# Spill transfers in 256 KB halves, last sums on half of the rows, fewer magnitudes on VectorE, and a new order

## The chip, the cores and the metric

One core of a Trainium2 chip runs the kernel: TensorE (PE in the profile), VectorE (DVE), ScalarE (ACT), GpSimd (POOL), and SyncE (SP), which here only issues transfers. The metric is the device time of one execution in microseconds. The time before is the median of three runs.

## What is computed

Two state-space convolutions, A and B, of one input u (2048 x 512), mixed by a gate. For each of 512 channels d, the kernel K is a sum over 128 complex states:

```python
    logdA = dt * A                     # A = A_re + 1j * A_im, dt = exp(log_dt)
    P = jnp.exp(logdA[:, :, None] * l[None, None, :])            # l = 0 .. 2047
    K = jnp.einsum("dn,dnl,dn->dl", Cc, P, dB).real
    ...
    Kf, Uf = rfft(K padded to 2L), rfft(u padded to 2L)
    y = irfft(Uf * Kf)[:L] + u * Dskip
...
x = A_u
g = sigmoid((x * gate_w).sum(-1, keepdims=True))
out = g * A_ref(x) + (1 - g) * B_ref(x)
```

(The names of the reference are kept; padding and transposes are shortened.)

## The kernel before

All of it is float32. The 512 channels are cut into 8 chunks of 64, and a chunk has 128 columns, 64 of model A and 64 of B. A column's kernel K over 2048 positions is the product of two small tables over the 128 states, 32 and 64 positions long, so that a matmul over the states makes K. The work has these stages.

- **Steps T = 0 to 63** (`tables`, lines 543 to 596), 16 columns each, 8 to a chunk. POOL makes integer angles (tile `ang`, two products) and magnitudes (tile `mr`: a large product of 64 positions from the seeds `ml`, lines 555 to 565, and a small one of 32 from `mh`, line 566). ACT takes two sines and a square of the angles into the PSUM tiles `s` and `sq`. DVE multiplies them with the magnitudes into `ei` (imaginary part) and `mr` (real part), four instructions. PE makes K from `mr` and `ei` (`kgen`, line 588, 64 matmuls as the profile counts them), ACT or DVE copies it to `kt`. The large magnitude product is on POOL, except in every third step (T % 3 == 2), where ACT copies the 8 x 16 seeds to a PSUM bank and DVE multiplies from there.
- **First stage of the transform** (`first`, line 605): after every second step, 32 matmuls of `kt` into two PSUM banks, copied into `xa` (even chunks) or `xb` (odd ones). The same is done with u itself (tile `uin`, `u_spectra`, lines 622 to 637), two chunks at a time; then the second stage of u's transform goes to tile `z` and is stored in DRAM as `us`: eight parts j a pair of chunks, one store of 512 KB for each two parts.
- **Product** (`conv`, lines 674 to 694): for each chunk and j = 0 to 7, SP loads u's spectrum (256 KB, tile `u`, three buffers; for the last chunk into `ml` and `mh`), PE makes the second stage of K's transform (line 618) and DVE multiplies both into `y` (line 690).
- **Way back** (`back`, lines 696 to 729): for each two parts, U = 0 to 3, 64 matmuls (line 710) into two banks, two copies x = 0, 1 into `z`, a store of 512 KB into the DRAM tile `zb` and a load of 512 KB from there into 32 of the 128 partitions of `f` (for the last chunk: `xa`). The way through DRAM turns positions into partitions. For U = 3 of the last chunk alone, both transfers were already cut in halves.
- **Last sums** (`fin`, lines 734 to 748): for each chunk, k = 0 to 3, 32 matmuls (line 742) of `f` with the gated matrices `gsi`; A and B are added in PSUM. A copy to `o` (two buffers) and an output transfer of 128 KB follow. Sum k reads the rows 8k to 8k + 7 of `f`.

Every operation is written with what it reads and writes (`Plan`, lines 153 to 198). The string `ORDER` (line 82) then lists all 1853 operations by number, in the order in which they are issued; a trailing `b` takes an operation's second engine (for a PSUM copy DVE instead of ACT, for the last outputs POOL's queue instead of SP's). Each engine works through its own operations in that order and waits where one isn't ready; so does SP with its transfers: one that waits holds up all behind it. A tile's buffers are taken in the order of the list, and an operation that opens a buffer waits for the last user of what was in it. There are four PSUM banks `c` for everything but the sines, and two buffers of `z` for stores.

The lines that the change touches: 555 (which steps), 631 to 637 (stores of u's spectrum), 685 (the loads' dependence), 716 to 729 (stores and loads of `zb`), 745 (what a last sum waits for), and the order.

Of the kernel before, what the change touches and what calls it, by code (L numbers as in the profile page):

```python
# [23 lines left out]
NB, NA = 64, 32  # L24
# [58 lines left out]
6 7 11 8 9 4 2 182 3 1 82 83 0 84 475 86 186 183 18 19 20 24 21 22 23 25 26 27 28 29 30 31 32 33 34 35 37 88 184b 185b 38 17  # L83
36 85 190 326 40 44 45 39 41 42 46 47 48 366 76 49 50 51 59 79 73 71 75 187 52 53 188 189 54 55 56 57 138 58 191 193b 61 62
67 63 60 68 192 64 69 91 14 351 87 13 218 194 15 16 98 65 70 92 93 101 94 95 89 96 43 72 66 353 77 354 78 90 74 100 99 195
102 357 104 103 105 219 113 197b 196b 198 200 355 356 221b 114 360 358 359 199 201 385 203 205 386 361 107 204 206 106 220
226 127 222 327 202 207 210 213 208 209 211 212 129 80 97 12 368 369 383 367 81 10 384 362 108 363 109 110 111 215 214 370
364 216 365 223 112 116 115 371 224 373 122 121 117 123 374 225 372 388 124 118 119 120 387 375 227 217 1403 230 125 126 128
131 134 376 228 389 136 133 231 352 132 137 135 130 5 1406 229 429 232 377 233b 244 390 378 245 391 392 393 249 394 251 395
430 250b 397 398 399 400 401 246 402 403 479 247 477 476 480 478 141 396b 404 405 406 142 143 239 144 252b 145 146 248 1414  # L90
253 148 149 234 150 151 152 407 254 240 431 416 414 427 415 154 139 140b 153 235b 155 236 418 408 379 419 420 409 237 483 417
421 422 428 410 445 446 447 147 448 241 242 156 157 432 380 381 423 159 424 435 158 436 411 433 434 437 413b 438 382 412 160
458 459 481 255 262 175 238 258 484 449 450 257 256 425 439 161 163 452 451 426 440 485 460 482 441 461 162 259 165 166 260
261 453 172 171 173 174 454 263 462 463 265b 167 164 455 168 169 612 611 464 264 609 613 177 266 179 243 176 328 330 331 290
329b 465 267 269b 268b 466 456 457 610 487 467 468 280 282 281b 469 283b 488 470b 294 284 486 170 180 499 501 616 489 502 490
491 492 471 500 442 493 518 519 516 517 494 472 444 443 503 504 495 496 506 332 275 505 473 474 531 333 507 508 520 521 509
276b 497 510 498b 522 511 532 523 524 529 533 530 277 285 278 287 270 272 286 534 535 288 525 526 536 547 549 550 548 512 537
538 334 335 608 279 289 527 336 551 539 540 552 271 553 560 562 561 554 555 528b 541 337 273 564 542 513 563 556 339 178 338
557 558 579 514 515 567 568 580 565 559 566 581 577 543 578 582 593 591 592 594 1407 1408 569 570 585 1404 544 586 583 546
584 545 340 587 588 1405 595 596 341 571 572b 598 342 1415 1426 614 618 615 573 619 599 1416 597 1425 617 181 1417 1409 1410  # L100
1411 274 1412 589 633 590 622 623 349 345 1427 600 1418 1419 601 574 602 575 576 624 603 620 621 649 347 343 625 634 626 1420
1429 635 631 632 651 652 604 348 650 744 1421 636 637 681 1428 1436 1450 1437 1422b 627 1430 628 1438 639 640 605 629 638 607
606 630 653 1413 1423 1424 1447 1439 1431 654 641 642 655 1432 643 656 657 658 662 663 664 665 666 644 679 680 645 659 695
667 1433 668 1448 660 1440 669 670 1449 682 1441 684 685 661 683 693 671 672 687 344 350 694 696 346 646 647b 1442 688 1443b
1444b 1434 1458 741 742 746 648 686 673 1459 745 674 743 1451 1435 1445 1461 689 690 691 1460 1452 692b 712 710 675 711 713
676 697 698 700 1453 701 699 678 677 714 1454 715 1455 1462 702 1446 703 717 704 1757 1763 705 725 1463 718 726 716 1764 1758
1483 1469 1470 719 723 727 724 747 751 749 706 753 754 748 752 728 729 1464 720 1471 1465b 750 1759 1765 1456 1480 1472 1466b
721 1760 1766 731 1761b 876 730 732 733 722 1767 1481 1473 878 755 707 1482 734 1474 735 708 783 709 756 757 736 1762 1457
1768 1475 1484 764 766 765 737 767 758 784 759 760 768 1476 769 1477 738 761 771 1485 740b 739b 772 770 773 1491 1467 1494
1468 1478 1502 762 1486 1487b 1488b 774 1495 1496 877 874 875 1492 1503 1493 775 785 781 795 814 782 796 815 786 763 787 776  # L110
# [3 lines left out]
835 836 810b 837 850 811 1776 848 851 1779b 856 857 849 838 852 879 858 839 883 859 880 853 860 885 886 861 1528 1519 882  # L114
1501 854 1529 862 1520 855b 863 864 1521 1010 840 884 887 897 899 900 898 1780 1777 1522 842 841b 865 1530 866 1531b 1532b
888 889 291 292 890 867 868 293 891 892 901 295 893 894 297b 296 902 869 914 916 915 904 917 870 905 903 871 872 1538 1523
298 299 918 302 1533 1534 1512 906 895 301b 907 303 921 922 305b 908 927 928 919 300 920 896b 304b 929 932 933 909 316 306
308 923 924 930 307b 309b 931 945 946 947 910 318 1784 925 935 317b 1785b 936 926b 1781 1007 934 1008 319 1009 1011 1782 977
310 937 938 978 323 321 322b 939 1786 320 1783 324b 325 1535 1006 1546 948 949 952 940b 958 959 960 961 1014 941 979 950 313
311 1790 1787 951 953 312 314 1791 962 954 975 976 911 955 965 1788 963 966 913 964 912 1539 1536 956 1540 967 989 968 942  # L120
957 980 943 981 982 1537 944b 983 991 990 1547 1548 984 1550 1541 985 1542b 986 1543b 315 1015 1549 1571 1557 1789 969 1551
1558 987 1144 1143 970b 993 1016 1012 1013 992 971 994 1559 988 995 996 997 998 972 974 973 1552 1031 1017 1020 1553 999 1032
1018 1554 1544 1560 1582 1033 1019 1029 1000 1021 1001 1561 1023 1024 1562 1572 1002 1030 1003 1022 1034 1025 1026 1573 1037
1035 1036 1005 1004 1027 1569 1047 1049 1048 1050 1060 1038 1545 1555 1579 1568 1792 1139 1556 1028 1051 1052 1563 1564 1565
1039 1040 1054 1583 1041 1053 1042 1062 1061 1043 1063 1093 1077 1094 1055 1570 1574 1580 1064 1065 1056 1067 1057 1575b
1576b 1044 1068 1584 1581 1046b 1566 1590 1140 1141 1066 1069 1142 1045 1058 1591 1059 1079 1070 1080 1592 1091 1078 1081
# [3 lines left out]
1103 1128 1275 1182 1129 1606 1130 1131 1132 1802 1613 1602 1120 1803 1133 1603 1614 1134b 1150 1104 1151 1162 1163 1152 1135  # L130
1164 1165 1153 1156 1154 1105 1801 1615 1589 1155 1107 1106 1157 1183 1179 1180 1158 1136 1607 1166 1137 1167 1138b 1169 1159
1170 1225 1608 1609 1168 1600 1623 1637 1610 1271 1616 1160 1624 1617 1184 1226 1625 1171 1618 1185 1273 1172 1619b 1620 1635
1173 1187 1634 1804 1188 1161b 1186 1272 1174b 1636 1276 1274 1626 1621 1611 1193 1227 1194 1195 1175 1196 1210 1211 1627
1176 1189 1190 1628 1191 1197 1178b 1200 1198 1177 1199 1629 1192b 1630 1631 1638 1201 1622 1648 1645 1202 1639 1203 1646
1811 1212 1213 1214 1215 1216 1812 1640 1641 1632 1670 1647 1217 1218 1219 1204 1649 1642 1220 1650 1223 1279 1224 1241 1242
1228 1231 1232 1229 1230 1814 1805 1808 1205 1809 1233 1243 1244 1254 1255 1656 1643 1813 1221 1245 1222 1246 1815 1206 1256
# [65 lines left out]
def ssm_mix(ctx: ExitStack, tc: tile.TileContext, a, out, dry=False):  # L202
# [419 lines left out]
    def u_spectra(b):  # L622
# [6 lines left out]
        for j in range(NJ):  # L629
# [205 lines left out]
```

## Time and profile before

| | us |
|---|---|
| three timed runs | 475.12, 477.8, 482.99 |
| their median | 477.8 |
| the profiled execution | 472.5 |
| its span, in which the trace's times lie | 470.7 |
| around the span | 1.8 |

The granted TensorE clock over the span is 0.971. PE is TensorE's matmuls, PEld its weight loads, SPq SyncE's queue. Transfers moved 84.5 MB, at 180 GB/s in the mean. Times of the trace count from the span's start.

### The profile page before, as it was taken

The numbers are of one execution on the slowest core, as the hardware profiler recorded it, in microseconds if no ns is written. First come the engines' busy times: TensorE is split into PE (matmuls) and PEld (weight loads), VectorE is DVE, ScalarE is ACT, GpSimd is POOL, SyncE is SP. The second block draws the span as 40 slices with busy tenths as digits, with TensorE's granted clock in tenths as the row PEclk, the third lists the DMA queues.
The fourth block names the chain that finished last, engine by engine and source line by source line (L and its number), as shares of the span: only waits on it lengthen the run. The fifth ranks groups of instructions, "written<-read, shape, count | busy, mean of one in ns | idle before, by whom it ended". The sixth has DMA issues, their size and how long they took to land.

```text
span 470.7 us, 21838 instructions
## 1 busy us (share of the span) xinstructions
PE 394.9 (84%) x9616; PEld 356.4 (76%) x9616; DVE 416.0 (88%) x518; ACT 386.2 (82%) x676; POOL 338.8 (72%) x317
## 2 busy tenths in 40 slices
PE   4797786799968879998898988879598888999935
PEld 3786685689857768787798977778587877898934
DVE  6999889999999999999899999998789999996610
ACT  3889979999988999998899999998789898791110
POOL 2593859599977989796999689878929899650010
PEclk9899899999998999999999999999999999999987
DMA  7866852836555565876465646764838667567793
GB/s 220 276 198 205 246 161 78 249 120 224 183 157 157 133 160 180 212 206 178 132 180 153 206 132 190 193 182 117 195 105 218 167 192 213 152 184 187 212 244 89
DMA packets 74542, 84.53 MB, mean 180 GB/s; under 512 B 5456, under 2 KB 60112, under 8 KB 73392
## 3 DMA queue, kind: packets, MB, share of 16 engines
q1 hardware_dynamic: 74304, 82.75, 62.0%
q8 instruction: 75, 1.23, 1.1%
q0 software_dynamic: 144, 0.39, 0.3%
q14 instruction: 19, 0.16, 0.1%
HBM read 51.48 MB, written 31.65 MB: 177 GB/s over the span
## 4 chain that ended last, share of the span: by engine, by line
PE 35%; DVE 25%; ACT 21%; issue 11%; DMA 4%; SPq 3%; DVEq 0%; POOL 0%; ACTq 0%
PE c L618 8%; PE c L605 8%; DVE mr L281 6%; PE c L588 6%; PE c L742 5%; PE c L710 4%; DVE y L690 4%; ACT s L284 4%; DVE ei L271 4%; ACT ang L284 3%; ACT sq L284 3%; SPq L289 3%; ACT ml L523 2%; DVE ei L281 2%; PE c L439 2%
## 5 line engine op out<-in xcount | busy, mean ns | idle before, releaser
L281 DVE SCALAR_TENSOR_TENSOR mr<-sq,mr 128x1024 f32<-128x1024 f32 (+1 forms) x128 | 117.4, 947 | 1.9 <-ACT sq L284 1.5
L271 POOL TENSOR_TENSOR mr<-ml 128x1024 f32<-128x1024 f32 x43 | 84.3, 1960 | 12.3 <-PE c L588 7.7
L271 POOL TENSOR_TENSOR ang<-par,cint 128x512 int32<-128x512 int32 x64 | 67.5, 1055 | 31.0 <-ACT sq L284 15.9
L271 DVE TENSOR_TENSOR ei<-s,mr 128x1024 f32<-128x1024 f32 x64 | 77.7, 1214 | 4.1 <-ACT s L284 2.8
L588 PE MATMUL c<-mr 128*32 128x64 f32 x2048 | 64.7, 223 | 14.8 <-DVE mr L281 7.3
L605 PE MATMUL c<-small,kt 128*64 128x128 f32 x1024 | 66.3, 283 | 10.9 <-issue 5.0
L690 DVE TENSOR_TENSOR y<-c,u 128x1024 f32<-128x1024 f32 x57 | 68.7, 1214 | 4.3 <-PE c L618 1.7
L284 ACT ACTIVATE s<-ang 128x1024 f32<-128x1024 int32 x64 | 65.9, 1029 | 6.5 <-POOL ang L271 4.5
L605 PEld LDWEIGHTS c<-small,kt 128*64 128x64 f32 x1024 | 58.2, 141 | 15.4 <-issue 6.3
L271 POOL TENSOR_TENSOR mr<-mh 128x512 f32<-128x512 f32 x63 | 67.7, 1080 | 2.4 <-PE c L588 2.4
L271 POOL TENSOR_TENSOR ang<-sa 128x512 int32<-128x512 int32 x64 | 68.6, 1073 | 0.2
L284 ACT ACTIVATE ang<-ang 128x1024 f32<-128x1024 int32 x64 | 67.7, 1058 | 1.2
L284 ACT ACTIVATE sq<-ang 128x1024 f32<-128x1024 f32 x64 | 66.0, 1032 | 3.2 <-DVE mr L281 2.3
L588 PEld LDWEIGHTS c<-mr 128*32 128x32 f32 x2048 | 48.6, 110 | 25.5 <-issue 9.9
L588 PE MATMUL c<-ei 128*32 128x64 f32 x2048 | 64.1, 221 | 3.2 <-issue 3.2
L710 PE MATMUL c<-y,vv 64*64 64x128 f32 x1792 | 59.9, 274 | 4.6 <-issue 2.7
L710 PEld LDWEIGHTS c<-y,vv 64*64 64x64 f32 x1792 | 50.9, 134 | 10.6 <-issue 5.2
L618 PE MATMUL c<-xa,w 128*128 128x128 f32 x384 | 52.8, 287 | 3.5 <-DVE vv L414 1.3
L618 PE MATMUL c<-xb,w 128*128 128x128 f32 x384 | 50.0, 282 | 4.7 <-DVE xb L296 1.3
L588 PEld LDWEIGHTS c<-ei 128*32 128x32 f32 x2048 | 50.6, 111 | 3.6 <-issue 3.6
L618 PEld LDWEIGHTS c<-xa,w 128*128 128x128 f32 x384 | 46.4, 194 | 7.7 <-issue 3.6
L618 PEld LDWEIGHTS c<-xb,w 128*128 128x128 f32 x384 | 45.1, 191 | 8.5 <-issue 3.1
(109 smaller groups left out, 661.9 us busy)
## 6 DMA issues: line engine op xcount, KB each, us to landing
zb<-z SPq DMA_DIRECT2D x31, 512.0 KB, 3.9
u<-us SPq DMA_DIRECT2D x57, 256.0 KB, 4.4
f<-zb SPq DMA_DIRECT2D x28, 512.0 KB, 5.2
us<-z SPq DMA_DIRECT2D x16, 512.0 KB, 3.7
uin<-in_uk_dram SPq DMA_DIRECT2D x16, 256.0 KB, 3.9
f<-in_ut_dram SPq DMA_DIRECT2D x8, 512.0 KB, 5.3
out_dram<-o SPq DMA_DIRECT2D x29, 128.0 KB, 3.2
par<-prd SPq DMA_DIRECT2D x7, 320.0 KB, 3.9
```

Of the source, the lines that this page charges most:

```text
L271: lambda e: (dve if e == "dve" else pool).tensor_tensor(out=out(), in0=in0(), in1=in1(), op=o),
L281: lambda _: dve.scalar_tensor_tensor(out=out(), in0=in0(), scalar=s, in1=in1(), op0=o0, op1=o1), reads, writes, port=port)
L284: op("act", "act", n, lambda _: act.activation(out=out(), in_=in_(), func=func, **{k: v() if callable(v) else v for k, v in kw.items()}), ...
L289: lambda e: (sp if e == "sp" else pool).dma_start(out=out(), in_=in_()), reads, writes, touch=touch)
L439: pe.matmul(t(*ps)[:, CH * i:CH * i + CH], V(x)()[:, CH * i:CH * i + CH], dgv()[:, k, i], start=True, stop=True)
L523: act.activation(out=t(*tile)[:, ks, j], in_=t("par", c)[:, 0, ks].bitcast(F32), func=AF.Exp, scale=float(l))
L588: pe.matmul(ps[32 * j:32 * j + 32, o], x[:, 4 * o + j, 64:96], x[:, 4 * o + j, 0:64], start=part == 0, stop=part == 1, tile_position=(0, 3 ...
L605: pe.matmul(t(*ps[g // 4])[64 * r:64 * r + 64, 128 * (g % 4):128 * (g % 4) + 128], t(*x)[:, g], t("small")[:, 128 * r:128 * r + 128], star ...
L618: pe.matmul(view()[:, :, k], t("w2", j // 2)[:, 4 * (j % 2) + k], t(*x1)[:, 4 * j + k], start=True, stop=True)
L690: op("dve", "tt1", 1024, lambda _: dve.tensor_tensor(out=t(*y).rearrange("p h s f d -> p h s (f d)"), in0=fv().rearrange("p s f d -> p s ( ...
L710: pe.matmul(bank_of(x)[64 * e:64 * e + 64, CH * q:CH * q + CH], v[:, 0:64] if h else v[:, 32:96], t(*ys[f // 4])[64 * x:64 * x + 64, h, :, ...
L742: pe.matmul(t(*ps)[64 * r:64 * r + 64, DC * i:DC * i + DC], t("gsi")[:, 4 * k + i, s, 64 * r:64 * r + 64], t(*f)[:, 8 * k + 2 * i + r, DC ...
```

## The change

Four things are changed.

1. Each store of u's spectrum, each store of `z` to `zb` and each load of `f` from `zb` becomes two transfers of 256 KB. A store's half leaves after its own copy x (or its own part j); a load of u's spectrum waits for its own part only; each half of a load of `f`, cut by rows (0 to 15, 16 to 31), waits for both halves of its store.
2. A last sum waits for those halves of the four loads that hold its rows: k = 0, 1 for the first ones, k = 2, 3 for the second.
3. The large magnitude product is on DVE in every fifth step (T % 5 == 4).
4. The order of all operations, now 1922, is a new one.

```diff
-        if T % 3 == 2:
+        if T % 5 == 4:
             sd = ("c", "seeds", T)
...
-            copy(512, zv, lambda ps=ps: t(*ps), [ps], [z])
-            if j % 2:
-                dma(512, lambda j=j: t("uspec", b, j // 2).rearrange("h p x -> p h x"),
-                    lambda z=z: t(*z).rearrange("p j f c -> p (j f c)").rearrange("p (h x) -> p h x", h=4), [z],
-                    [("uspec", b, j // 2)])
+            copy(512, zv, lambda ps=ps: t(*ps), [ps], [z] * (1 - j % 2) + [("uz", b, j)], touch=[z] * (j % 2))
+            dma(256, lambda j=j: t("uspec", b, j // 2)[2 * (j % 2):2 * (j % 2) + 2].rearrange("h p x -> p h x"),
+                lambda z=z, j=j: t(*z)[:, j % 2].rearrange("p f c -> p (f c)").rearrange("p (h x) -> p h x", h=2), [("uz", b, j)],
+                [("uspec", b, j)], touch=[z])
...
-        us = ("uspec", c // 2, j // 2)
+        us, stored = ("uspec", c // 2, j // 2), ("uspec", c // 2, j)
...
-        for xs in ((0,), (1,)) if end else ((0, 1),):
-            g, n = 8 * U + 4 * xs[0], 4 * len(xs)
-            dma(128 * n // 2, lambda g=g, n=n: t(*zb)[g:g + n].rearrange("g p k -> p g k"),
-                lambda xs=xs: t(*z)[:, xs[0]:xs[-1] + 1].rearrange("p x q k -> p (x q) k"),
-                [("zx", c, U, x) for x in xs], [zb] * (U == 0) + [("zu", c, U)], touch=[z] + [zb] * (U > 0))
-        for h in range(1 + end):
-            m = NA // (1 + end)
-            dma(16 * m, lambda h=h, m=m: t(*f)[32 * U:32 * U + 32, m * h:m * h + m],
-                lambda h=h, m=m: t(*zb)[8 * U:8 * U + 8].rearrange("g (m a) k -> (g m) a k", m=4)[:, m * h:m * h + m],
-                [("zu", c, U)], [f] * (U == 0) + [("fu", c, U, h)], touch=[zb] + [f] * (U > 0))
+        new = U == 0
+        for x in range(2):
+            g = 8 * U + 4 * x
+            dma(256, lambda g=g: t(*zb)[g:g + 4].rearrange("g p k -> p g k"), lambda x=x: t(*z)[:, x],
+                [("zx", c, U, x)], [zb] * (new and x == 0) + [("zu", c, U, x)], touch=[z] + [zb] * (not (new and x == 0)))
+        for h in range(2):
+            dma(256, lambda h=h: t(*f)[32 * U:32 * U + 32, 16 * h:16 * h + 16],
+                lambda h=h: t(*zb)[8 * U:8 * U + 8].rearrange("g (m a) k -> (g m) a k", m=4)[:, 16 * h:16 * h + 16],
+                [("zu", c, U, 0), ("zu", c, U, 1)], [f] * (new and h == 0) + [("fu", c, U, h)],
+                touch=[zb] + [f] * (not (new and h == 0)))
...
-        op("pe", "fin", 64, mm, [("gsi", k)] + [("fu", c, U, 0) for U in range(4)] + [("fu", c, 3, 1)] * (c == NCH - 1 and k > 1),
-           [ps], table="fin", touch=[f])
+        op("pe", "fin", 64, mm, [("gsi", k)] + [("fu", c, U, k // 2) for U in range(4)], [ps], table="fin", touch=[f])
```

What the two lists give each engine, counted from the numbers:

| | before | after |
|---|---|---|
| large magnitude products on POOL / on DVE | 43 / 21 | 52 / 12 |
| copies of seeds on ACT | 21 | 12 |
| transfers on SP / on POOL | 250 / 3 | 329 / 2 |
| copies to `o` on ACT / on DVE | 26 / 6 | 23 / 9 |
| copies to `z` on ACT / on DVE | 68 / 28 | 70 / 26 |
| copies to `xb` on ACT / on DVE | 33 / 15 | 32 / 16 |
| changes of ACT between exponential and sine | 30 | 28 |

The end of the two lists, SP's transfers of the last chunk with x or h in brackets (outputs left out before the last store). Before: store U=2, store U=3 (0), load U=1, store U=3 (1), then load U=2, load U=3 (0), load U=3 (1), and outputs. After: load U=0 (0), load U=0 (1), load U=1 (0), stores U=2 (0), (1), stores U=3 (0), (1), load U=2 (0), load U=1 (1), load U=3 (0), an output, load U=2 (1), an output, load U=3 (1), and outputs. The last two copies into `z` are both DVE's before, and ACT's and DVE's after. The last matmuls keep their sequence: products and ways back of the last chunk, with sums of the chunk before it among them, and four sums of its own at the end.

More of the change, by code (lines that the diff above doesn't have):

```diff
@@ new lines @@
+378 379 109 110 208 125 16 15 129 226 200 203 230 209 206 210 211 213 214 402 97 386 380 381 387 216 219 217 220 111 112 115
+116 389 390 113 114 121 117 122 227 123 124 118 80 399 400 119 388 228b 403 229 404 391 392 231 233 232b 215 127 212 343 221
+234 126 235 237 393 405 394 431 236b 250 251 120 412 414 415 413 135 218 128 131 132 368 406 407 408 253 256 254b 409 432
+257b 259 410 416 411b 419 420 417 130 252 133 134 136 255 495 260 418 491 238 239 492 494 141 493 148 144 421 142 422 143 423
@@ new lines @@
+149 1410 137 151 145 146 266 261 262 258 1423 240 424 150 152 139 153 140b 154 429 433 443 430 434 437 155 247 244 241 462
+395 444 445 425 446 147 164 438 435 245 436 248 242 447 396 397 156 157 448 439 440 449 163 450 451 158 460 498 461 426 428b
+427 398 464 452 453 263 160 159 161 473 463 474 496 175 270 499 264 265 441 454 465 442 455 466 162 267 165 166 268 269 467
+468 171 172 173 174 469 456 497 500 475 476 502 477 274 243 249 246 177 176 271 275 470 273b 272b 276b 471 480 167 481 472b
@@ new lines @@
+1033 984 1035 1598 985 1599 1044 1013 1057 1059 1060 1058 1036 1037 1606 1607 1047 1014 1016b 1048 1045 1600 1046 1038 1015
+1089 1039 1061 1062 1049 1050 1611 1063 1612 1051 1622 1072 1070 1071 1052 1621 1577 1017 1618 1601 1064 1065 1066 1090 1074
+1075 1613 1631 1591 1590 1858 1632 1619 1623 1067 1620 1633 1053 1073 1091 1054 1068 1614 1602 1647 1615 1634 1644 1616 1603
+1149 1151 1056 1076 1150 1069 1624 1635 1087 1088 1103 1077 1078 1079 1080 1055b 1625b 1636 1092 1081 1648 1093 1082 1095
@@ new lines @@
+1626 1865 1096 1649 1094 1097 1101 1102 1104 1156 1105 1866 1120 1083 1121 1118 1119 1637 1084 1098 1106 1638 1108 1109 1099
+1107 1110 1100b 1111 1639 1086 1122 1173 1085 1123 1578 1657 1604 1617 1871 1862 1660 1627 1867 1628 1640 1645 1125 1863b
+1126 1131 1132 1133 1154 1112 1646 1124 1872 1135 1113 1136 1157 1864 1868 1127 1128 1174 1284 1114 1115 1116 1137 1134 1138
+1139 1869b 1117b 1129 1658 1140 1158 1155 1159 1162 1130 1141 1659 1650 1142 1661 1160 1161 1163 1164 1165 1166 1143 1651
+1171 1172 1144 1175 1191 1189 1652 1176 1177 1145 1167 1662 1168 1179 1180 1641 1629 1642 1643 1873 1670 1654 1673 1280 1653
@@ L150 @@
+1405b 1379b 1762 1733 1746 1888 1761 1777 1891 1747 1758 1757 1763 1406 1407 1767 1408 1409b 1775 1768b 1776 1778 1779 1769
+1791 1788 1780 1781 1759 1771 1770 1734 1772 1773 1782 1783 1784 1760 1792 1789 1801 1804 1793 1817 1814 1805 1802 1806 1818
+1815 1794 1795 1796 1901 1807b 1902b 1808b 1797 1785 1786 1798 1809 1810 1903b 1819 1820 1907 1904 1898 1821b 1905b 1899 1822
+1823 1811 1799 1824 1906 1812 1900 1908b 1825 1909 1910 1913 1911 1914 1912b 1915 1916 1919 1917 1920 1918 1921
 """
@@ L685, in conv @@
         dma(256, lambda: uv().rearrange("p h f d -> p (h f d)"),
-            lambda: t(*us)[2 * (j % 2) + c % 2].rearrange("(q h) x -> q (h x)", h=2).unsqueeze(1).to_broadcast([64, 2, 512]), [us], uk + over)
+            lambda: t(*us)[2 * (j % 2) + c % 2].rearrange("(q h) x -> q (h x)", h=2).unsqueeze(1).to_broadcast([64, 2, 512]), [stored], uk + over)
         fv = lambda: t(*fw).rearrange("p (s f d) -> p s f d", s=2, f=4)
@@ L715, in back @@
         z, zb, f = ("z", c, U), ("zb", c), home(c)
-        end = last and U == 3
         for x in range(2):
```

85 lines of the change are left out of this document (29 added, 56 removed), and 30 rows, old and new, of the table ORDER.

## The prediction

> **What bounds the kernel now.** I read the page's busy line first, then busy time by stretch, the waits, the groups of instructions, the issues of transfers, and last the chain that ended last.
>
> ```profile
> span 470.7 us, 21838 instructions
> PE 394.9 (84%) x9616; PEld 356.4 (76%) x9616; DVE 416.0 (88%) x518; ACT 386.2 (82%) x676; POOL 338.8 (72%) x317
> ```
>
> DVE is the fullest engine, but 88% is a mean over stages that differ. Busy time in the two stretches that matter, the steady part from the ninth step's tables to the last one's, and the end (length, then busy time of PE, PEld, DVE, ACT, POOL with counts, granted clock, DMA share, GB/s):
>
> ```profile
> 102.00:425.00 323.00, 285.69 (x7596) 256.43 (x7594) 307.76 (x354) 294.96 (x491) 271.50 (x244) 0.98 0.62 172
> 425.00:471.00 46.00, 31.91 (x752) 29.82 (x752) 16.77 (x19) 6.65 (x14) 2.00 (x4) 0.89 0.70 184
> ```
>
> In the first DVE is busy 307.8 of 323 us and idles 15.2 us; ACT is at 91%, PE at 88%, POOL at 84%. So for 323 us DVE sets the pace with three engines close behind it. In the second DVE and POOL have nearly nothing left: after the last step's tables, 46 us remain that are a chain of matmuls and transfers. DVE's few idle times come from these waits:
>
> ```profile
> DVE xb L296 <- PE c L605: 5.1, 1, 5.1
> DVE ei L271 <- ACT s L284: 2.8, 4, 1.8
> DVE y L690 <- DMA u<-us: 0.6, 2, 0.4
> ```
>
> The third is the one that the transfers touch: with 64 products that each need a u load, DVE lost 0.6 us to loads that came late. The first is one single stall, looked at under the rivals.
>
> **The change part by part.**
>
> *Magnitudes.* A step's product mr<-ml runs on DVE in every third step (21 of 64) and on POOL in the others (43). With every fifth it is 12 and 52. Each product on DVE also needs a small ACT copy of the seeds into a PSUM bank. The groups (busy us, mean ns, idle before):
>
> ```profile
> L271 POOL TENSOR_TENSOR mr<-ml 128x1024 f32<-128x1024 f32 x43 | 84.3, 1960 | 12.3 <-PE c L588 7.7 <-ACT ml L523 1.7 <-issue 1.1
> L271 DVE TENSOR_TENSOR mr<-c,ml 128x1024 f32<-128x1024 f32 x21 | 25.5, 1214 | 1.5 <-ACT c L284 1.5
> L284 ACT ACTIVATE c<-ml 128x128 f32<-128x128 f32 x21 | 5.9, 281 | 0.1
> ...
> L296 DVE COPY o<-c 128x256 f32<-128x256 f32 x6 | 2.5, 417 | 17.2 <-DMA out_dram<-o 9.8 <-PE c L742 7.5
> L296 DVE COPY xb<-c 128x512 f32<-128x512 f32 x15 | 10.0, 680 | 5.2 <-PE c L605 5.1
> ```
>
> DVE loses nine products. One is 1.214 us by the group, but back to back a DVE product of that size takes less, as the chain shows:
>
> ```profile
> 125.09 1.13 DVE ei L271
> ```
>
> So 9 x 1.13 = 10.2 to 9 x 1.214 = 10.9 us come off DVE. The new order also deals the PSUM copies anew between ACT and DVE: three more o and one more xb on DVE, two spill copies fewer (the size of xb): 3 x 0.417 + 0.680 - 2 x 0.680 = +0.6 us. DVE's net is -9.6 to -10.3 us; I take -9.6, since the steady stretch runs back to back. POOL gets 9 x 1.96 = +17.6 us, ACT loses 9 x 0.281 = 2.5 us.
>
> *The order, ACT's tables.* Going down the two lists, ACT changes between its exponential and its sine tables 30 times before and 28 times after. Two loads less:
>
> ```profile
> L284 ACT ACT_TABLE_LOAD x18 | 23.1, 1283 | 1.0 <-PEq L824 0.7
> ```
>
> 2 x 1.283 = 2.6 us off ACT. By itself neither this nor the seeds' copies move the end: ACT is not the last to be waited for. It is cover for the next point.
>
> *The balance that is left.* Put on the steady stretch: DVE 307.8 - 9.6 = 298.2, POOL 271.5 + 17.6 = 289.1, ACT 295.0 - 2.5 - 2.6 = 289.9, PE 285.7 us as before. DVE still has the most, but POOL has come from 36 us below it to 9 us below. If DVE's idle time stayed at 15.2 us the stretch would lose the whole 9.6. If POOL set the pace with the same idle time, 289.1 + 15.2 = 304, it would still be shorter than 313, so POOL does not become the bound by its sum; it can only be late for single steps. When POOL is late ACT's sine waits first, and DVE behind ACT:
>
> ```profile
> ACT s L284 <- POOL ang L271: 4.5, 6, 1.8
> ```
>
> The bounds for what the tighter balance costs are 0 (all as now) and 9.6 us (everything given back). Nearest is DVE's wait on ACT's sine above, 2.8 us in 4 times with POOL at 84%; with POOL at 289.1/313 = 92% I let it double and charge +2.8 us. Steady stretch: -9.6 + 2.8 = -6.8 us.
>
> *Transfers of the spills in halves.* The 16 stores us<-z become 32; of 32 stores zb<-z and 32 loads f<-zb all but the last chunk's last pair, which is halved already, become two: 62 more. With one output moved from POOL to SP, SP issues 79 more. Issue times in ns with the landings of this tile's transfers, and the page's list of issues (count, size, median us to landing):
>
> ```profile
> L289 SPq DMA_DIRECT2D zb<-z x33: 359/376/1365, 134.7 to 451.2; - x33
> L289 SPq DMA_DIRECT2D f<-zb x28: 312/356/1414, 141.9 to 436.6; - x28
> ...
> DMA to landing us min/median/max: 3.2/4.9/7.5
> ```
>
> ```profile
> zb<-z SPq DMA_DIRECT2D x31, 512.0 KB, 3.9
> u<-us SPq DMA_DIRECT2D x57, 256.0 KB, 4.4
> f<-zb SPq DMA_DIRECT2D x28, 512.0 KB, 5.2
> ...
> zb<-z SPq DMA_DIRECT2D x2, 256.0 KB, 4.5
> xa<-zb SPq DMA_DIRECT2D x2, 256.0 KB, 5.2
> ```
>
> A half issues in the same time (33 stores, both sizes, 0.36 to 0.38 us from fastest to median) and lands no sooner (4.5 against 3.9, 5.2 against 5.2). So 79 x 0.38 = 30 us more of SP, which computes nothing, and no round trip gets shorter by size. What is won is the start: the first half of a spill leaves one copy earlier (0.68 us for one of xb's size on DVE, above). What is risked: SP issues strictly in order, and each half of an f load waits for both halves of its store; behind it stand u loads for DVE and outputs that free the o buffers. I cost all this at nothing, covered by the slack that DVE's 0.6 us wait for u shows. If that cover goes, it is the third rival.
>
> *First last-sums from the first half of the rows.* Sums k = 0, 1 of a chunk wait only for the first halves of f. For the seven chunks ahead of the last, these sums are PE filler with no one close behind: zero. For the last chunk this was already so for its last spill, which is the last to come: zero, too.
>
> *The tail.* The end of the chain (start, us, what):
>
> ```profile
> 448.69 1.30 DVE z L296 x2
> 449.99 0.51 SPq L289
> ...
> 451.16 5.34 DMA zb<-z
> ...
> 456.89 4.33 DMA xa<-zb
> 461.21 5.94 PE c L742 x128
> ```
>
> The two last copies run one after the other on DVE, 1.30 us; in the new order one is ACT's and one DVE's: 0.68, so -0.6. From the copies' end to the last store's start SP needs 451.16 - 449.99 = 1.17 us, as an earlier f load stands between the two stores; in the new order they follow one another: -0.5. Ahead of them stands f(U=1), which waits for its store to land; that store leaves four matmul groups earlier, so this is covered unless it lands late. The second half of the last f load stands three issues behind the first, 4 x 0.38 = 1.5 us, while the sums of the first half take 5.94/2 = 3.0: hidden. Two transfers in series and the 5.94 us of matmuls stay. The tail gives -1.1 us. Its other bound is +2.6: the store in front lands in this tile's maximum, 7.5, instead of its median, 4.9.
>
> *The head.* Loads come in another order, PE's and DVE's work listed ahead of the first step's tables, summed with the rows' means, is about 2 us less than before, and the loads arrive no earlier, so 0, with bounds of -2 and +2.
>
> **Sum.** -6.8 - 1.1 + 0 = -7.9 us. The profiled execution took 472.5 us (470.7 of span, 1.8 around it); it would take 464.6. The three timed runs lie at 475.1 to 483.0, median 477.8, 5.3 above the profiled one; I set the sum on the median: 477.8 - 7.9 = 469.9, about 470 us.
>
> **The rivals.**
>
> *A. All of it, and the stall too.* In the midst of 64 matmuls of the first stage PE stood 4 us with no wait:
>
> ```profile
> 333.58 2.19 PE c L605 x36
> 335.77 4.02 issue
> ```
>
> ```profile
> q8 instruction: 75, 1.23, 1.1%
> ```
>
> DVE's 5.1 us above is this stall's shadow. The instruction queue moved 75 packets, 1.23 MB; what such a packet meets among the data transfers depends on the order, so another order may not have it. With 10.3 of DVE, 5.1 and 1.1 that is 16.5 us: 461.3. For it: it happened once. Against it: more, smaller transfers are in flight in the same stretch (DMA share 0.62). The Trainium skill, page "Runtime: NRT & Kernel Launch", section "Instruction fetch mechanics", says that an engine refills its instructions in 16 KiB blocks and that the crossing is mostly hidden. 1.23 MB over 75 is 16.4 KB and agrees with the block; the 4.02 us do not agree with hidden, and by the page's rule alone this rival would be the forecast.
>
> *B. POOL takes back what DVE gives.* POOL works in order, and its four products of a step stand against the pace of the steps:
>
> ```profile
> L271 POOL TENSOR_TENSOR ang<-sa 128x512 int32<-128x512 int32 x64 | 68.6, 1073 | 0.2
> L271 POOL TENSOR_TENSOR mr<-mh 128x512 f32<-128x512 f32 x63 | 67.7, 1080 | 2.4 <-PE c L588 2.4
> L271 POOL TENSOR_TENSOR ang<-par,cint 128x512 int32<-128x512 int32 x64 | 67.5, 1055 | 31.0 <-ACT sq L284 15.9 <-DMA uin<-in_uk_dram 8.6 <-PE c L588 5.8
> ```
>
> ```profile
> L271 DVE TENSOR_TENSOR ei<-s,mr x64: 1209/1212/1226, 28.8 to 421.3; 128x1024 f32<-128x1024 f32 x64
> ```
>
> That is 1.07 + 1.08 + 1.06 + 1.96 = 5.2 us against (421.3 - 28.8)/63 = 6.2 a step. If each of the nine moved products makes its step's sine late by one POOL product of 1.07 us, and DVE with it, 9 x 1.07 = 9.6 us come back and the steady part gains nothing: with the tail 476.7. For it: 92%. Against it: POOL waits 15.9 us for ACT to free an angle buffer (the releaser in the third row), so it mostly runs ahead and has room.
>
> *C. Slower: SP's queue makes u late.* One mechanism: a u load stands behind one more issue or a half that waits, DVE's product waits, and DVE sets the pace. At 0.38 us for each of 64 products it costs 24.3 us: 477.8 - 7.9 + 24.3 = 494.2. At 0.12 us each the gain is gone, at 0.27 (17.5 us) the kernel is 2% slower. Against it: 0.6 us now, and in the new list DVE's work between a u load and its product, summed with the rows' means, has a median of 7.0 us, against 5.7 before. The Trainium skill, "DMA: Bandwidth & Descriptors", section "Anatomy of one DMA — SWDGE (gpsimd) path", gives about 2.0 us fixed for a transfer plus its bytes over 436 GB/s: an estimate of 3.2 us for 512 KB and 5.2 for two halves in series, so 78 halved transfers would carry 156 us more latency. The rows have no such gap, since the halves overlap.
>
> **How the numbers follow.** The forecast (466 to 474, middle 470) gets 0.46; A (459 to 466) 0.24; B (474 to 482) 0.19; C (over 482) 0.11. About 2%, 9.6 us, is what a measurement of this kernel can tell from no change: under 468.2 or over 487.4. Faster: A and a third of the forecast, 0.24 + 0.16 = 0.40. Slower: most of C, 0.08. Within: 0.52. The range 461 to 482 leaves out a quarter of A and C, 0.06 + 0.11; the forecast's own is 466 to 474.
>
> **What would show it.** In the steady part: DVE's mr<-c,ml x12 and POOL's mr<-ml x52 at the same means; DVE busy near 406, its idle time there near 18 us. If DVE's waits on ACT's sine or on POOL stay at 3 us, my charge was too high; near 12 us, B is right. DVE's wait for u<-us above 8 us means C. No issue stall of 4 us means half of A. In the tail: two z copies side by side, the last store's start within 1 us of the last inverse group's copies. The forecast is wrong if DVE's busy time falls by ten and the last step's tables do not end earlier.

## The result, and the profile after

The changed kernel takes 460.8 us (median; 456.7 to 462.8) where the kernel before takes 476.5 (470.5 to 483.0) in the same comparison: a ratio of 0.971 [0.966, 0.976]. Every ratio in this text (with its 95% interval) leaves out the runs over 1.5% above the fastest of their kernel, and as the runs of the kernel before spread widely, most ratios are a little above those of the medians (0.967 here). The kernel is faster, by twice what was forecast, and 0.2 us outside the range. The profiled execution took 461.8 us, 460.0 of it span; against the profiled one of before the span lost 10.7 us. That execution of before (472.5) lay near the fast end of its runs.

From the page of the changed kernel: span, busy time, the instruction queue, and the issues of transfers.

```profile
span 460.0 us, 21963 instructions
...
PE 394.3 (86%) x9616; PEld 356.7 (78%) x9616; DVE 408.9 (89%) x511; ACT 379.3 (82%) x663; POOL 355.7 (77%) x325
...
q8 instruction: 75, 1.23, 1.2%
...
zb<-z SPq DMA_DIRECT2D x64, 256.0 KB, 3.6
u<-us SPq DMA_DIRECT2D x57, 256.0 KB, 3.9
f<-zb SPq DMA_DIRECT2D x56, 256.0 KB, 4.7
us<-z SPq DMA_DIRECT2D x32, 256.0 KB, 3.4
```

DVE has 7.1 us less, POOL 16.9 more, ACT 6.9 less, where the forecast had 9.6 less, 17.6 more and 5.1 less. In the median each kind of spill transfer lands sooner than the 512 KB before (3.6 for 3.9, 4.7 for 5.2, 3.4 for 3.7 us), and so do the u loads between them, whose size did not change (3.9 for 4.4).

Busy time in the same two stretches as before, from the ninth step's tables to the last one's, and the end:

```profile
102.40:417.70 315.30, 283.00 (x7589) 254.10 (x7587) 299.48 (x342) 289.80 (x483) 285.44 (x251) 0.98 0.64 180
417.70:460.00 42.30, 31.58 (x744) 29.69 (x744) 16.33 (x20) 6.66 (x14) 1.46 (x3) 0.90 0.69 196
```

The steady stretch is 7.7 us shorter (323.0 before), the end 3.4 (45.7 from 425.0 to the span's 470.7), the head the same (102.4 for 102.0). The forecast had 6.8, 1.1 and 0. The steady part seems to come out nearly as forecast; the experiments show that this is chance, as it comes from another place.

That place shows best in the 4.02 us in which PE stood amid 64 matmuls at 335.77 us before. At this point of the program the changed kernel has (PE's instructions in order: start, us, what)

```profile
332.75 1.97 PE L607 MATMUL c<-small,kt 128*64 128x128 f32 x32
334.65 1.98 PE L711 MATMUL c<-y,vv 64*64 64x128 f32 x64
```

with no gap. The page tells what it was. PE has 9616 matmuls and 9616 weight loads, 19232 instructions; over the 75 packets of the instruction queue that is 256 each, and 1.23 MB over 75 is 16.4 KB. In the traces PE's gaps without a wait lie at every 256th of its instructions. So PE gets its instructions by DMA in blocks of 256 and stands where a block is late. The trace's records of single packets show it: ahead of each of the ten gaps of over 0.8 us before, a packet of 16,384 bytes of the instruction queue ends 1.3 to 1.5 us before PE goes on. I measure this as PE's *fetch loss*: at each 256th instruction that lies within one operation, the time from the start of the instruction ahead of it to its own, less the usual 0.03 us, summed up over the gaps that are longer than that. Before it is 19.6 us, in sixteen gaps of over 0.3 us and many small ones; after it is 8.5. The 4.02 us of the forecast's rival A were only the largest of them.

At that largest gap the packets also show what the DMA engines did meanwhile. Two loads f<-zb had been issued one behind the other, and from 332.5 to 336.5 us their packets of 16 KB hold 15 to 16 of the 16 engines. The instruction packet starts at 337.08 us, as they end, takes 1.35 us (the median of all is 1.09), and PE goes on 1.37 us later. So the packet was not slow, it started late. One thing stays open: PE had entered its last block at 329.0 us, and around 331.2 us only some 3 engines were busy; why the next block was not fetched then the trace does not show.

All kernels that ran, with the loads f<-zb as they are requested for one spill, their median landing, the fetch loss and its largest gap, the profiled span, the median, and the ratio to the kernel before in the same comparison:

```
kernel                        f requests     landing  loss  max  span   median  ratio
before                        512 KB           5.2    19.6  4.3  470.7  476.5
the change                    2 x 256          4.7     8.5  2.7  460.0  460.8   0.971 [0.966, 0.976]
after_again                   2 x 256          4.7     9.2  2.1  458.6  459.9   0.978 [0.974, 0.983]
after_third                   2 x 256          4.5     8.6  1.8  457.6  461.1   0.981 [0.974, 0.989]
old order, old magnitudes
 halves_old_order             2 x 256          4.3    10.9  1.7  460.4  467.3   0.990 [0.983, 0.996]
 f_halves_old_order           2 x 256          4.3    15.2  1.8  465.0  471.3   0.992 [0.986, 0.997]
 stores_halved_old_order      512              5.3    20.2  5.0  474.0  474.3   1.000 [0.994, 1.006]
 f_packets_old_order          512, 8 KB        5.5    24.2  3.1  475.1  478.2   1.007 [0.999, 1.015]
 f_by_partition_old_order     2 x 256          6.2    31.1  7.9  497.8  502.7   1.060 [1.049, 1.071]
 f_quarters_old_order         4 x 128          3.2     9.2  1.5  463.1  464.7   0.979 [0.975, 0.982]
 f_cut_old_order              32               2.5     6.5  1.6  461.5  463.2   0.977 [0.973, 0.981]
 quarters_halves_old_order    4 x 128          3.5     7.7  2.2  460.6  464.0   0.989 [0.985, 0.994]
old order, new magnitudes
 mags_old_order               512              5.3    18.8  2.4  476.5  479.6   1.020 [1.016, 1.025]
 mags_and_halves_old_order    2 x 256          4.3    10.4  1.7  469.8  472.8   0.999 [0.995, 1.003]
new order, new magnitudes
 whole_new_order              512              6.1    12.6  3.3  478.4  482.7   1.026 [1.021, 1.032]
 f_halves_new_order           2 x 256          4.6     9.9  2.4  463.2  464.9   0.982 [0.977, 0.988]
 f_quarters_new_order         4 x 128          3.5     4.7  1.5  459.7  459.9   0.970 [0.959, 0.980]
 quarters_new_again           4 x 128          3.7     6.9  2.0  457.9  460.2   0.980 [0.972, 0.987]
 outs_free_new_order          2 x 256          4.9     7.1  2.3  460.2  460.7   0.973 [0.967, 0.979]
```

The kernel before, in the five further comparisons, has medians of 476.7, 476.8, 474.3, 475.1 and 474.3 us, and its runs spread over 7 to 15 us. Differences under some 3 us between kernels of different comparisons decide nothing.

### The profile page after: what moved, and what is told of

Read it like the earlier page. It is cut to its first block, busy times and chain, and to the rows that moved or that the text cites. A ratio compares the mean times of both kernels' runs of the same rounds, so it can differ in the third digit from the quotient of the medians.

```text
span 460.0 us, 21963 instructions
## 1 busy us (share of the span) xinstructions
PE 394.3 (86%) x9616; PEld 356.7 (78%) x9616; DVE 408.9 (89%) x511; ACT 379.3 (82%) x663; POOL 355.7 (77%) x325
## 3 DMA queue, kind: packets, MB, share of 16 engines
q8 instruction: 75, 1.23, 1.2%
## 4 chain that ended last, share of the span: by engine, by line
DVE 26%; PE 23%; ACT 16%; issue 11%; DMA 11%; POOL 9%; SPq 3%; DVEq 0%; ACTq 0%; POOLq 0%
PE c L620 7%; PE c L607 6%; DVE mr L283 6%; DVE ei L273 5%; POOL mr L273 4%; PE c L590 4%; ACT s L286 3%; DVE y L691 3%; POOL ang L273 3%; DMA out_dram<-o 3%; PE c L711 3%; SPq L291 3%; ACT sq L286 2%; ACT ang L286 2%; DMA u<-us 2%
## 5 line engine op out<-in xcount | busy, mean ns | idle before, releaser
L273 POOL TENSOR_TENSOR mr<-ml 128x1024 f32<-128x1024 f32 x52 | 101.8, 1958 | 4.7 <-PE c L590 2.9
L711 PE MATMUL c<-y,vv 64*64 64x128 f32 x1792 | 58.1, 273 | 4.1 <-DVE y L691 1.4
L620 PE MATMUL c<-xa,w 128*128 128x128 f32 x384 | 51.3, 283 | 2.5 <-ACT z L296 1.1
L620 PEld LDWEIGHTS c<-xa,w 128*128 128x128 f32 x384 | 45.4, 191 | 6.6 <-issue 1.5
```

The source lines that it names most:

```text
L273: lambda e: (dve if e == "dve" else pool).tensor_tensor(out=out(), in0=in0(), in1=in1(), op=o),
L620: pe.matmul(view()[:, :, k], t("w2", j // 2)[:, 4 * (j % 2) + k], t(*x1)[:, 4 * j + k], start=True, stop=True)
L711: pe.matmul(bank_of(x)[64 * e:64 * e + 64, CH * q:CH * q + CH], v[:, 0:64] if h else v[:, 32:96], t(*ys[f // 4])[64 * x:64 * x + 64, h, :, ...
```

## The experiments

### One part at a time

First the change again, unaltered.

> The changed kernel once more, unaltered, for the spread of a profile. In the changed kernel's trace PE loses 8.5 us at its instruction refills (gaps at every 256th instruction, beyond the usual spacing), in the kernel before 19.6 us, and the spans differ by 10.7 us. Theory H (halved transfers shorten the refills' waits) and theory O (the new order happens to have fewer of them) both expect 461 us +- 3 and 6 to 12 us of such gaps. If the gaps are chance from one execution to the next, this run shows 15 us or more.

459.9 us: it holds. Then the change taken apart. The halves alone, in the old order and at the old places:

```diff
-            dma(16 * m, lambda h=h, m=m: t(*f)[32 * U:32 * U + 32, m * h:m * h + m],
+            dmas(16 * m, [(lambda k=k: t(*f)[32 * U:32 * U + 32, 16 * k:16 * k + 16],
...
+                           for k in ((0, 1) if not end else (h,))],
```

and the same for the stores us<-z and zb<-z: one operation of the list issues both halves, one behind the other.

> The kernel before in its own order, with each 512 KB store us<-z and zb<-z and each 512 KB load f<-zb issued as two of 256 KB at the same place. Theory H: PE's gaps at the refills fall from 20 us to about 9, and the time from 476.5 to about 466. Theory O: gaps stay near 20 us, time 476 +- 3. If more issues on SP cost anything: above 480.

467.3 us, 9.4 below before (476.7 in this comparison), where the change is 16.8 below. What the forecast costed at nothing is more than half of the gain. Busy time in the steady stretch, in the columns of above:

```profile
102.40:416.80 314.40, 282.66 (x7599) 253.36 (x7599) 307.41 (x354) 294.42 (x491) 271.52 (x244) 0.99 0.63 177
```

DVE has all of its work of before (307.4 us, 307.8 before) and idles 7.0 us in place of 15.2; its wait of 5.1 us for PE's stall is gone. Then the reverse, the new order with whole transfers; a store goes out at the place of its later half, a load at that of its earlier one:

```diff
-            dma(256, lambda h=h: t(*f)[32 * U:32 * U + 32, 16 * h:16 * h + 16],
+            once(("f", c, U), 0, 256, lambda: t(*f)[32 * U:32 * U + 32],
```

> The changed kernel in its new order, with the halves of a spill joined again into one transfer of 512 KB (a store at the place of its later half, a load at that of its earlier one). Theory H: gaps at the refills rise from 9 us to about 20, time about 471. Theory O: gaps near 9 us, time 461 +- 3, or up to 2 us more for the later stores.

482.7 us, slower than before, and outside what either theory had. Its fetch loss is only 4 us above the change's, so the larger part of these 22 us is something else: the order was made for halves, f's loads land after 6.1 us, and SP's queue stands longer behind DVE's products. Its largest wait (us in total, times, longest), first with whole transfers, then in the change:

```profile
SPq L291 <- DVE y L705: 86.4, 28, 11.8
```

```profile
SPq L291 <- DVE y L691: 55.6, 25, 8.7
```

These waits may be a cause or a mark of the lateness; that was not parted here.

Last, the magnitudes alone in the old order: nine of the 21 products go to POOL in their places.

```diff
-        if T % 3 == 2:
+        if T in (5, 11, 17, 26, 32, 38, 47, 53, 59):
+            tt("any", G * 64, lambda: t(*M)[:, :, 0:64].rearrange("p c (h l) -> p c h l", l=8),
...
+        elif T % 3 == 2:
```

> The kernel before in its own order, with 9 of the 21 large magnitude products moved from DVE to POOL at the same place and their copies of the seeds left out; transfers whole. Theory M (fewer products on DVE shorten the steady part, as the prediction had it): DVE's busy time 406, time 476.5 - 7 = 469 or less. Theories H and O: the steady part has enough other waits that less than 3 us comes of it, 474 to 478.

479.6 us, slower by 2% and above what every theory had: DVE has 8.2 us less to do, and the kernel takes longer. Where each of these gains or loses is seen in the times at which DVE ends the tables of step T (from the traces, us):

```
T     before  halves_old  f_cut_old  mags_old  mags_and_halves  the change
8     102.0   102.4       102.9      101.1     102.8            102.4
12    119.1   119.5       120.0      120.9     122.6            119.5
32    244.5   242.9       243.6      245.9     246.3            244.0
44    315.1   314.2       314.2      317.5     318.2            314.8
48    345.4   338.1       337.8      347.2     344.6            335.2
63    424.9   416.8       416.3      430.4     424.8            417.7
```

At T = 44 before, the halves and the change stand within a us of each other, whatever DVE has had to do. Between T = 44 and 48, where PE's largest fetch gap of before lies, the halves gain 6.4 us, and they hold them to the end of the tables. The kernel with the magnitudes alone is 1.8 us behind before at T = 12 and 5.5 at T = 63. In this execution the change has gained nothing over the halves alone at T = 63 (in its two other profiled ones 2.7 and 1.4 us).

### Which transfers, and which property

The loads alone in halves, and the stores alone:

> The kernel before in its own order; only the 512 KB loads f<-zb are halved, by rows of f, so that a packet has 8 KB instead of 16 KB. Theory P (a refill of PE's instructions waits behind the 16 KB packets of these loads, 1.12 us each on a DMA engine): as good as all transfers halved, about 467 us, at most 2 refills that start more than 4 us late, against 5 before. Theory S (it is the stores, or the smaller transfers as a whole): half of the gain or less, 472 to 477.

> The kernel before in its own order; only the stores us<-z and zb<-z are halved, their packets keep 512 bytes and 1 KB. Theory P: no gain, 476 us +- 3, 4 to 6 refills more than 4 us late. Theory S: 467 to 472.

471.3 and 474.3 us, where before has 476.8: the loads carry the larger part, with a ratio clear of 1, the stores' ratio is 1.000. The loads' 471.3 us lies between the two theories. Now a load in halves of 16 partitions instead of 16 rows, so that its packets stay at 16 KB:

```diff
-            dma(16 * m, lambda h=h, m=m: t(*f)[32 * U:32 * U + 32, m * h:m * h + m],
+            dmas(16 * m, [(lambda k=k: t(*f)[32 * U + 16 * k:32 * U + 16 * k + 16],
```

> The kernel before in its own order; the loads f<-zb are halved by partitions, 16 and 16, so that there are as many transfers of 256 KB as with rows halved, but each packet keeps 16 KB. Theory P: no gain, 476 us +- 3, 4 to 6 late refills. Theory T (the size of a transfer is what matters, not of its packets): about 467.

502.7 us, 26 us slower than before. I had not expected that. The chain of work through its largest fetch gap (start, us, what):

```profile
344.12 1.10 PE c L595 x64
345.23 2.19 PE c L612 x34
347.41 7.59 issue
355.01 2.18 PE c L612 x17
```

It is the matmul group of before's stall (x36, then 4.02 us), and the same place with 7.6 us. In the halves by rows PE goes through that group without a stop:

```profile
330.68 3.79 PE L612 MATMUL c<-small,kt 128*64 128x128 f32 x64
```

In the kernel by partitions, too, the 16 KB packets of these loads hold the DMA engines at that place, 15 to 16 of them from 345.2 to 351.2 us, and the instruction packet starts at 351.59. The packets' own times show why such loads block for longer (median us of one packet on a DMA engine, loads f<-zb and xa<-zb):

```
before           16 KB   1.12      f_halves    8 KB  0.59
f_by_partition   16 KB   1.79      f_packets   8 KB  0.61
whole_new_order  16 KB   1.19      the change  8 KB  0.48
```

So far a packet's length and a request's size could both be it. To tell them apart, a load of 512 KB as one request, with packets of 8 KB: the halves of a row of `f` lie apart in the tile, so that they cannot merge.

```diff
-    ring("f", 1, [128, NA, CH])
+    ring("f", 1, [128, NA * CH + 8])
...
+                lambda: t(*f)[32 * U:32 * U + 32].rearrange("p (h x) -> p h x", h=2)[:, :, 0:16 * CH],
```

> The kernel before with one thing changed: the two halves of a row of f lie 32 bytes apart in SBUF, so that a load f<-zb is still one transfer of 512 KB in its old place, but of 64 packets of 8 KB in place of 32 of 16 KB (the loads of the last chunk go to xa and stay as they were). Theory P (what costs is how long one packet holds a DMA engine, and PE's instruction fetch behind it): the gain of the halved loads, 476.7 to 471, comes without any halving: 470 to 473 us, at most two refills that start over 4 us late, PE loses 16 us or less at them. Rival R (the gain came from two transfers that are requested and land on their own): as before, 475 to 479 us, five or six late refills, some 19 us lost.

(The halves lie 16 bytes apart, 32 for the whole tile, not 32 apart as the expectation says.) 478.2 us, ratio 1.007: nothing gained, 24.2 us lost at the fetches. My theory of the packet's length fell. For loads into 32 partitions it is the request that counts: the same bytes in packets of the same length, asked for twice, gain 5 us. The page's issues of this kernel, and those of the halved loads:

```profile
f<-zb SPq DMA_DIRECT2D x28, 512.0 KB, 5.5
```

```profile
u<-us SPq DMA_DIRECT2D x57, 256.0 KB, 4.1
f<-zb SPq DMA_DIRECT2D x56, 256.0 KB, 4.3
```

The Trainium skill, page "DMA: Bandwidth & Descriptors", section "Queues, rings and completion order", says that each DMA engine takes turns between its queues by whole packets, a packet there being a run of descriptors from one ring (the profile calls each descriptor a packet). That agrees with the pair above: an instruction block waits for an engine's whole share of a request, four 8 KB pieces of 0.61 us in one request or twice two of 0.59. The traces don't say on which engine a packet ran, so this stays an agreement and is not shown, and at the largest gap of before it does not suffice, as the instruction block came behind two whole requests. The load by partitions does not follow from it alone: its share of an engine is one packet of 1.79 us, less than the whole load's two of 1.12, and its loss is the largest.

If so, still smaller requests lose still less, and a load without its bytes loses nearly nothing. Both in the old order:

> The kernel before with each load f<-zb requested as four of 128 KB, one behind the other at the old place (packets of 4 KB; those of the last chunk to xa too). Theory Q (the size of a request is what counts, down to this size): PE loses 13 us or less, 466 to 470 us, less than the halves' 471. Rival H (the gain is had with two requests, and four cost SP more issues): 15 us lost as with halves, 470 to 474 us.

> The kernel before with the bytes of the loads f<-zb taken away and their places kept: each brings the first two of its 32 columns (32 KB in place of 512 KB; the last chunk's loads to xa are whole). The final matmuls of the other chunks read those two columns again and again, so that seven eighths of the output are not the reference's. Theory F (the fetches are late behind these loads, and PE's loss there counts one for one): PE loses 11 us or less, at most one fetch over 4 us late, span near 450 plus the loss, median 460 to 467 us. Rival W (the loads only go along with it; other transfers or the fetch itself are slow): some 19 us lost, five late fetches, 473 to 478 us.

Quarters: 464.7 us against 475.1, loss 9.2, below the 466 to 470 that the theory had. Cut, with 32 KB of each load's 512: 463.2, loss 6.5, in its range. The quarters stand within 2 us of a kernel whose loads bring hardly anything. But loss and time do not go one for one down to there, as that expectation had it: 450 and 6.5 are 456.5 us, and the span is 461.5. The busy line of the cut kernel's page:

```profile
span 461.5 us, 21838 instructions
...
PE 391.6 (85%) x9616; PEld 353.6 (77%) x9616; DVE 415.8 (90%) x518; ACT 385.1 (83%) x676; POOL 338.7 (73%) x317
```

DVE has all of its old work, and the span is within 1.5 us of the change's. Over the kernels of the old order and magnitudes, the one by partitions left out, loss and span fall together: 24.2 us with 475.1, 20.2 with 474.0, 19.6 with 470.7, 15.2 with 465.0, 10.9 with 460.4, and below some 10 us of loss the span stays at 460 to 463.

### What the new order and the magnitudes are worth

> The order of before with all spill transfers in halves (467.3 us) and nine magnitudes moved from VectorE to GpSimd in place (alone: 479.6, slower). Theory I (the removed VectorE work pays once PE's refills no longer stall the chain): 467.3 less the 6.8 us of the forecast, 460 to 462 us, and the new order is then worth nothing. Theory O (moving them in place costs as much here as it did alone, and what after has beyond the halves is the new order): 468 to 471 us, and the order is worth 8 to 10 us.

472.8 us, just above what the second theory had. With the smaller fetch loss (10.4 us), too, the moved magnitudes cost in place (+9.4 us of span to the halves alone), although DVE has 9 products less. DVE's waits in this kernel (us in total, times, longest):

```profile
DVE ei L271 <- ACT s L284: 7.4, 8, 2.2
DVE mr L281 <- ACT sq L284: 5.0, 10, 1.1
...
DVE ei L271 <- POOL mr L271: 2.5, 2, 1.9
```

With the halves alone there is no third one, and the others are

```profile
DVE mr L281 <- ACT sq L284: 1.5, 5, 0.5
DVE ei L271 <- ACT s L284: 1.4, 5, 0.4
```

The table above has the first 3 us of it at T = 12, right behind the first moved steps: POOL's product comes late, ACT's sine behind it, DVE last. ACT's sine waits 9.9 us for POOL's angles, 4.1 with the halves alone. That is the forecast's rival B. The new order gives these losses back. Then the loads in halves with whole stores, in the new order:

> The changed kernel with the stores us<-z and zb<-z joined to 512 KB again, each at the place of its later half; the loads f<-zb stay in halves. Theory P (the loads' packets carry most of what the halves give): 461 to 465 us, at most two refills over 4 us late. Rival S (the new order needs the early half stores, and their joining alone made 482.7 of 460.8 when all was joined): 472 to 483 us, with waits for zb and us on SP that after does not have.

464.9 us: 4 us above the change, and 18 below the whole transfers of the same order. So the 22 us of whole_new_order lie mostly in the loads. And quarters there:

> The changed kernel in its order, with each half of a load f<-zb issued as two quarters of 4 KB packets. Theory P: no more than 1 refill over 4 us late, PE's loss at the refills from 8 us to 4 to 6, the time 457 to 460. If the 64 further issues on SP cost more than that saves: above 462.

459.9 us, the change's own. The last comparison puts them on one chip:

> The order and the magnitudes of before, the loads f<-zb requested as four of 128 KB and the stores us<-z and zb<-z as two of 256 KB, all at the old places. Theory N (the transfers' requests are the whole gain; the new order and the moved magnitudes give nothing of their own): 459 to 462 us, equal to after within 0.5%. Theory O (the order and the magnitudes bring some more): 463 to 466 us, 3 us or more above after.

> The changed kernel, unaltered, on the chip of the run of quarters and halves in the old order, for the comparison: 459 to 462 us.

> The changed kernel with each half load of f requested as two of 128 KB, on the same chip. Theory Q (PE's loss at its fetches still counts, though less): 0 to 3 us below after. Rival B (something else, VectorE above all, now sets the pace): equal to after within 0.3%, though PE loses 4 us less.

464.0, 461.1 and 460.2 us, with 474.3 before. Old order and old magnitudes with small requests stand 2.9 us above the change: between the two theories, nearer to the one that gives the order some 3 us. That is the rest beside loads in quarters; beside the halves, the requests that the change itself has, it is 7.4 us (467.3 and 459.9 in one comparison). How the new order comes by it was not parted. Smaller requests add 0.9 us at most to the new order, within the spread, though the loss falls from 8.6 to 6.9 us.

### The end

The two `o` buffers seemed to hold the changed kernel's end: its last copies waited for outputs. So the last six outputs got places of their own, and the last loads go ahead of two outputs in SP's queue.

> The changed kernel with a freer end: the last chunk's four output tiles lie in f and the two before them in a table tile that is done, in place of the ring of two, and the two output DMAs that SP issued between the last loads xa<-zb come behind them. Theory E (the end is held by two output buffers and by SP's order): last matmul some 0.9 us earlier, copies no longer wait for out_dram, 457 to 459 us. Rival (the last loads and the last output's own flight set the end): 460 to 462 us.

460.7 us, no gain. The chain of this kernel's end:

```profile
442.26 3.82 DMA zb<-z
...
446.15 4.56 DMA xa<-zb
...
450.81 6.15 PE c L742 x128
```

Store, load, matmuls: with the outputs out of the way these remain, and 6.15 us of matmuls are no shorter. In the change the chain read "out_dram", but the matmuls were as late beside it.

## Why the prediction was wrong, point by point

- **Transfers of the spills in halves: the step that failed.** It was costed at nothing, since a half "lands no sooner" and "no round trip gets shorter by size", and it is more than half of the gain: 9.4 of 16.8 us by itself in the old order, ten by quarters of the loads alone. The step read a transfer's cost from its own landing and from SP's queue. It left out what a large request keeps from others on the same DMA engines, above all PE's instruction blocks. Even its own premise was drawn from the last spill, two stores and two loads: over all of them, halves land 0.3 to 0.9 us sooner.
- **Rival A** named the stall and gave 461.3 us for the sum with it, 0.5 from the result. That it comes so near is luck, as 10.3 us of this sum are DVE's, and those did not come. Its reason was half right: it held the stall for an accident of the order that "happened once". It was 19.6 us in many gaps, and the request's size takes most of them away without another order (10.9 with the halves alone). The order has a share: with whole transfers the new one loses 12.6 us, with halves 8.5. Its "against", more and smaller transfers in the same stretch, pointed the wrong way. The Trainium skill's rule there ("Runtime: NRT & Kernel Launch", "Instruction fetch mechanics") agrees with the trace on the block of 256 instructions. That crossing it is mostly hidden holds by number, sixteen gaps of over 0.3 us for 75 blocks, but these cost most of 19.6 us before, and 6.5 us are lost even with the loads' bytes cut.
- **Magnitudes, and the balance that is left.** The counts (52 and 12 products) and the time of one were right, DVE's busy time fell by 7.1 us in place of 9.6:

```profile
L273 POOL TENSOR_TENSOR mr<-ml 128x1024 f32<-128x1024 f32 x52 | 101.8, 1958 | 4.7 <-PE c L590 2.9 <-issue 1.6
L273 DVE TENSOR_TENSOR mr<-c,ml 128x1024 f32<-128x1024 f32 x12 | 14.6, 1215 | 0.0
```

  The gain of 6.8 us did not come from them: the halves alone, with DVE's old work, have a steady stretch of 314.4 us, the change 315.3. Against the halves, DVE is busy 7.9 us less there (299.5) and idle 8.8 us more (15.8). DVE's waits in the change:

```profile
DVE mr L283 <- ACT sq L286: 5.2, 13, 0.9
DVE ei L273 <- ACT s L286: 4.0, 3, 2.0
...
DVE ei L273 <- POOL mr L273: 1.7, 4, 0.8
...
DVE y L691 <- DMA u<-us: 0.6, 2, 0.3
```

  The first three rows here are 10.9 us over the span; in before the sine's is 2.8 and the square's

```profile
DVE mr L281 <- ACT sq L284: 1.5, 5, 0.6
```

  The charge for the tighter balance was +2.8 and measured +6.6; it left the square's wait out. In the steady stretch DVE's products also wait 3.8 us for PE's second stage, 1.0 before, and so DVE's gain is gone. Rival B was right in that the moved products gain nothing in the steady part, its mechanism holds only in part: in the old order it is at work, but in the change ACT's sine waits 4.8 us for POOL's angles, hardly more than the 4.5 before, and 9.0 us for DVE to be done with the last step's sine (`ei`), 1.8 before. What in the new order makes the sine and the square late was not tried.
- **Rival C** did not come: DVE waits 0.6 us for u, as before, with 79 more issues on SP. The figure quoted there from the Trainium skill ("DMA: Bandwidth & Descriptors", "Anatomy of one DMA — SWDGE (gpsimd) path") is for transfers that GpSimd issues, and these are SP's; halves landed sooner than whole ones, as said.
- **The order and ACT's tables; the first last-sums; the head.** The head moved by 0.4 us: right. The order with the magnitudes is worth 7.4 us beside halves and some 3 us beside quarters; what of it is the last-sums' part was not tried.
- **The tail** gave 3.4 us, not 1.1. The last store landed in 3.7 us in place of 5.34, and the halves alone have 2.1 of it (43.6 us).
- **The median.** The sum was set on a median of three runs. The profiled spans differ by 10.7 us, the medians by 15.7: before's runs reach to 483 us and the change's only to 462.8. That the stalls vary from run to run would fit; single runs beside the profiled ones have no trace.

## What to carry to other kernels

Look for idle time of an engine that waits for nothing, and at its spacing: at every 256th instruction it was here the engine's own instruction fetch, and then the DMA requests in flight are to be looked at, not the engine. A large load that nobody waits for can cost more than its landing shows; here it paid to split its request (not only its packets, and not by partitions), and it is worth measuring that alone before the order of the work is touched. And when a sum comes out about right, test one term by itself: here the right number stood on the wrong term.

## What the runs showed of the hardware that I had not expected

- An instruction packet took 1.09 us in the median, but at the largest gap of before it started only when two loads of 512 KB were nearly through, and PE stood for 4.3 us.
- The same 8 KB packets cost PE 24.2 us in requests of 512 KB and 15.2 in requests of 256 KB.
- A load into 16 partitions has packets of 16 KB that take 1.79 us each; into 32 partitions 1.12 us. In both some 16 are under way at a time. The two loads of a spill into 16 partitions each took some 4.6 us together from the first packet to the last, one whole load into 32 partitions 3.2, and the kernel took 26 us more. Why the packets are slower was not tried.
- Below some 10 us of fetch loss the span no longer follows it: 4.7 us of loss and 8.5 gave 459.7 and 460.0 us.
